# Where the second gate's logits are formed: all 18 row tiles on TensorE, and one table fetch moved behind the writes it reads

## The chip, the cores and the metric

The kernel runs on one core of one Trainium2 chip. The metric is the device time of one execution in microseconds; the time before is the median of three runs. A core has five instruction streams: TensorE (PE, with its weight loads as PEld), VectorE (DVE), ScalarE (ACT), GpSimd (POOL) and SyncE (SP, which issues most DMAs). Each takes its own instructions in the order in which they were issued, and waits at an instruction until what it needs is there.

## The reference, cut to what matters

Three layers follow one another on 2304 rows of 512 values: linear attention, a gated layer of 1536 hidden values, and a mixture of 8 experts of which each row takes one. The change is in the gate of the third layer and in the first expert's rows:

```python
gate = 1.0 / (1.0 + np.exp(-(x @ w_gate)))       # second layer
x = (gate * (x @ w_val)) @ w_out
logits = x @ w_gate                              # third layer: 2304 x 512 by 512 x 8
expert_idx = np.argmax(logits, axis=1)
gate_w = softmax(logits)[np.arange(N), expert_idx]
# rows go to their expert in order, at most `capacity` of them
h = np.maximum(np.einsum('ecd,edf->ecf', disp, w1), 0.0)
y = np.einsum('ecf,efd->ecd', h, w2)
out[i] = gate_w[i] * y[expert_idx[i], pos[i]]
```

## The kernel before, in words

Rows are worked on in six blocks (0 to 5) of 384, each three tiles of 128 rows. Every large product is three matmuls, of a high and a low part of its two operands (`mm3`).

**The loop of the second layer.** A step takes one block and two of the twelve hidden chunks. For each chunk TensorE forms the gate's and the value's sum (`gg` into tile `pg`, `gv` into `pv`), ScalarE the sigmoid (`gs`), VectorE the product with the value (`gm`, L483, tile `sg`), ScalarE and GpSimd its high and low parts (`hh`, L487, and `hl`, L491, tile `h`). Between the two chunks of a step TensorE multiplies the step before's `h` by the output weights (`g2`, tile `po`), and VectorE adds the sums to the rows (L521, tile `acc`) or leaves them open in PSUM for one more step. The last twelve of these steps are called step 0 to 11 here. Block 0 is complete in step 3, block 1 in step 4, block 2 in step 6, block 3 in step 8, block 4 in step 10 and block 5 right behind the loop.

**The gate of the third layer.** A complete block gets its logits, one number for each row and expert. Blocks 0, 1, 2 and two tiles of block 4 get them as sums of products over the row: VectorE sums five of the eight experts itself (`lg_dve`, L557, tiles `jk` and `lg`), GpSimd multiplies the other three (`lg_pool`, L564, tile `jp`) and ScalarE sums them (`lg_sum`, L570). A queue hands these out in steps 3 to 10 (`slot`). Block 3, the last tile of block 4 and block 5, 7 tiles, go to TensorE: `columns` (L780) transposes a row tile in four pieces into `pl`, ScalarE copies it to `w5` (L784), and `logits_mm` (L792, tile `plg`) multiplies by the gate's weights, a few of these matmuls behind each `mm3` of the next chunk (`weave`). Then `route` (L625 to L632) finds each row's expert, `route_b` (L644 to L673) its place in a table with two small matmuls (`pc`) and some twenty small operations of VectorE, and `put` scatters three tiles of entries into the table `tbl` in DRAM (GpSimd, L144). `choose` (L683 to L694) picks the first expert behind block 3, and the first expert's weights (`es`) are fetched from there on.

**Behind the loop** the first expert begins: 192 rows of blocks 0 to 3, gathered in step 10, are multiplied in eight chunks f = 0 to 7, while block 5 is routed (`after0`). Its other 384 rows are gathered at f = 4, and their table rows (`tb`, L160, token and gate weight of each) are used when the results are scaled and scattered at that part's end.

What sets the order of the work around the change is the order in which the code issues it: `at_step(k, j, ...)` puts work at step k, "s" and "t" ahead of the first and the second chunk's matmuls, "m" ahead of `g2`, 0 and 1 behind the first and the second chunk.

Of the kernel before, what the change touches and what calls it, by code (L numbers as in the profile page):

```python
# [8 lines left out]
F32 = mybir.dt.float32  # L9
# [9 lines left out]
P = 128  # L19
# [4 lines left out]
NE = 8  # L24
# [17 lines left out]
# The order in which the work up to the first pair of hidden chunks is issued, each engine's in turn: a step and  # L42
# what it is for (batch, tile or hidden chunk), with a star where VectorE takes it from its usual engine.
# [29 lines left out]
def program(tc, ins, outs):  # L73
    nc = tc.nc
    ctx = ExitStack()
    with ctx:
# [78 lines left out]
        def fetch(st, key, e, r0, k, rest=False):  # L155
            """The table's rows from r0 on: k to a partition, the rest's last half tile in both halves."""
            st[key] = t = tbp.tile([P, k + rest, 4], I32, name=key, tag=key[:2])
            t3 = tbl.rearrange("(e r) w -> e r w", e=NE)
            r1 = r0 + k * P
            nc.sync.dma_start(t[:, :k], t3[bass.ds(e, 1), r0:r1].rearrange("o (p k) w -> (o p) k w", k=k))  # L160
            if rest:
                for h in (0, HALF):
                    rows = t3[bass.ds(e, 1), r1 : r1 + HALF].rearrange("o p w -> (o p) w")
                    nc.sync.dma_start(t[h : h + HALF, k], rows)
# [23 lines left out]
        def part(x, w, sizes, ew, t, ypool, ytag, hook, after):  # L188
            """The rows of one table for one expert. The high and low parts of a tile of half the rows fill the
            array's columns together; the low part's sums then move to the high part's partitions."""  # L190
# [70 lines left out]
        with ExitStack() as s2:  # L261
# [249 lines left out]
            def g2(b, fs, mode):  # L511
                """mode: add (whole sums to SBUF), open and close (a sum over two pairs in PSUM)"""
                order = [(tt, i) for tt in range(TPB) for i in range(2)]
                if b == NBLK - 1 and mode == "close":
                    order = [(tt, 0) for tt in range(TPB)] + [(tt, 1) for tt in range(TPB)]
                for tt, i in order:
                    if i == 0 and mode != "close":
                        otile[b, tt] = pso.tile([P, 512], F32, name=f"po{b}_{fs[0]}_{tt}", tag="o")
                    pair(b, tt, fs[i], i, mode != "close" and i == 0, mode != "open" and i == 1)
                    if i == 1 and mode != "open":  # L520
                        nc.vector.tensor_tensor(row(b, tt), row(b, tt), otile[b, tt], op=ALU.add)  # L521
                if fs[-1] == NFC - 1:
                    finish(b)
# [6 lines left out]
            def open_routing():  # L530
# [3 lines left out]
                wg = p.tile([P, NE, DM], F32, name="wgb", tag="wgb")  # L534
                nc.sync.dma_start(wg, ins["wg"].rearrange("e d -> (e d)").unsqueeze(0).to_broadcast([P, NE * DM]))
                rt["wg"] = wg
# [4 lines left out]
                fill = p.tile([P, NROW // P, 4], I32, name="fill", tag="jp", bufs=2)  # L541
# [12 lines left out]

            def lg_dve(b, tt, e):
                junk = rt["pool"].tile([P, DM], BF16, name=f"jk{b}_{tt}_{e}", tag="junk")
                nc.vector.tensor_tensor_reduce(  # L557
                    junk, row(b, tt), rt["wg"][:, e, :], 1.0, 0.0, op0=ALU.mult, op1=ALU.add,
                    accum_out=rt["lg", b][:, tt, e : e + 1],
                )  # L560

            def lg_pool(b, tt, e):
                prod = rt["pool"].tile([P, DM], F32, name=f"jp{b}_{tt}_{e}", tag="jp", bufs=2)
                nc.gpsimd.tensor_tensor(prod, row(b, tt), rt["wg"][:, e, :], op=ALU.mult)  # L564
                acts.append((b, tt, e, prod))

            def lg_sum(keep):
                while len(acts) > keep:
                    b, tt, e, prod = acts.pop(0)
                    nc.scalar.activation(prod, prod, AF.Copy, accum_out=rt["lg", b][:, tt, e : e + 1])  # L570

            acts, qd, qg, ready = [], [], [], []
            nsum = {0: (5, 5, 5), 1: (5, 5, 5), 2: (5, 5, 5), 4: (5, 5)}

            def logits(b):
                """Queues the logits of block b: DVE sums nsum[b] products of a row, Pool and ScalarE the others."""
                lg_tile(b)
                for tt, n in enumerate(nsum[b]):
                    qd.extend((b, tt, e) for e in range(n))
                    qg.extend((b, tt, e) for e in range(n, NE))  # L580

            def slot(room, spare):
                """Fills the time that DVE (room, in products) and Pool (spare) have until the next pair's turn."""
                lg_sum(0)
                put = None
                busy = {x[0] for x in qd + qg}
                for b in [b for b in range(3) if ("lg", b) in rt and b not in busy]:
                    route(b)
                    ready.append(b)
                    room -= 2  # L590
                    break
                else:
                    if room > 4 and ready:
                        put = route_b(ready.pop(0))
                        room, spare = room - 5, spare - 3
                while room > 0 and qd:
                    lg_dve(*qd.pop(0))
                    room -= 1
                while spare > 0 and qg:
                    lg_sum(1)  # L600
                    lg_pool(*qg.pop(0))
                    spare -= 1
                if put is not None:
                    put()
# [171 lines left out]

            def columns(b, tt):
                pt = ps(f"pl{b}_{tt}")
                for c in range(NC):
                    nc.tensor.transpose(pt[:, c * P : (c + 1) * P], row(b, tt)[:, c * P : (c + 1) * P], ident)  # L780
                if tt == 1 and b == NBLK - 1:
                    nc.vector.tensor_copy(w5[:, 0, tt], pt)
                else:
                    nc.scalar.copy(w5[:, 0, tt], pt)  # L784

            def logits_mm(b, tts, then=None):
                if tts[0] == 0:
                    lg_tile(b)
                pl = ps(f"plg{b}")

                def one(tt, c):
                    nc.tensor.matmul(  # L792
                        pl[:, tt * NE : (tt + 1) * NE],
                        w5[:, 0, tt, c * P : (c + 1) * P],
# [5 lines left out]
                def end():  # L800
                    s = slice(tts[0] * NE, TPB * NE)
                    nc.vector.tensor_copy(rt["lg", b].rearrange("p t e -> p (t e)")[:, s], pl[:, s])
                    if then is not None:
                        then()

                n = 2 if b == 3 else 3
                pairs = [(tt, c) for tt in tts for c in range(NC)]
# [25 lines left out]
            for b, k in ((0, 3), (1, 4), (2, 6), (4, 10)):  # L833
                at_step(k, 0, lambda b=b: logits(b))
            for k in range(3, 9):
                at_step(k, 0, lambda k=k: slot(9 if k > 3 and k % 2 else 7, 5))
                at_step(k, 1, lambda: slot(4, 2))
            at_step(8, 1, lambda: [columns(3, tt) for tt in range(TPB)])
# [3 lines left out]
            at_step(9, "s", lambda: logits_mm(3, range(TPB), lambda: route(3)))  # L842
            at_step(9, "m", lambda: late("put2", lambda: route_b(ready.pop(0))))
            at_step(9, 0, lambda: rt["put2"](), choose, dma(0), dma(1), lambda: late("put3", lambda: route_b(3)))
            at_step(9, 1, lambda: rt["put3"]())
            at_step(10, 0, first_table, split(0), dma(2), lambda: slot(6, 5))
            at_step(10, "t", lambda: weave.extend([lambda: None] * 4 + [lambda: columns(4, 2)]))
            at_step(10, 1, lambda: slot(4, 1), split(1), dma(3), first_rows)
            at_step(11, "s", lambda: logits_mm(4, [2]))
            at_step(11, 0, lambda: lg_sum(0), lambda: route(4), split(2), dma(4))  # L850
# [3 lines left out]
            for i, (b, fs, mode) in enumerate(steps):  # L854
# [28 lines left out]
                if i == n4 + 7:  # L883
                    w5 = unit([P, 2, TPB, DM], F32, "w5")
# [17 lines left out]
            def last_rows():  # L902
# [12 lines left out]
                def end():  # L915
# [3 lines left out]
                    rt["put"]()  # L919

                weave.extend([lambda: None] + [lambda k=k: one(k) for k in range(3)] + [end])

            def after0(f):
                if f == 0:
# [4 lines left out]
                    logits_mm(b5, range(TPB), lambda: route(b5))  # L929
# [6 lines left out]
                if f == 3:  # L936
                    last_rows()
                    ew_split(ew0, 7, both)
                    fetch(st0, "tb", rt["e0"], R0, 3)
# [119 lines left out]
def layout(inputs):  # L1059
# [14 lines left out]
    wg = np.ascontiguousarray(inputs["moe2_w_gate"].T)  # L1074
    wgt = np.ascontiguousarray(inputs["moe2_w_gate"].reshape(NC, P, NE).transpose(1, 0, 2))
    cap = np.asarray(inputs["moe2_capacity"]).astype(np.int64).reshape(1)
    return {"q": q, "v": v, "kT": kT, "w": w, "w1": w1, "w2": w2, "wg": wg, "wgt": wgt, "cap": cap}
# [20 lines left out]
```

## Time and profile before

| | us |
|---|---|
| median of three runs | 813.92 |
| lowest and highest | 813.45, 814.21 |
| span of the profiled execution, first to last instruction | 815.9 |
| TensorE busy in that span | 757.5 (93%) |
| VectorE, GpSimd, ScalarE busy | 474.4 (58%), 321.0 (39%), 293.0 (36%) |

The profile is of one execution, and its time is given by the span alone; that is 2.0 us above the median. TensorE is busy nearly throughout, so the places to read are those in which it isn't, and what it waits for there.

### The profile page before, as it was taken

The numbers are of one execution on the slowest core, as the hardware profiler recorded it, in microseconds if no ns is written. First come the engines' busy times: TensorE is split into PE (matmuls) and PEld (weight loads), VectorE is DVE, ScalarE is ACT, GpSimd is POOL, SyncE is SP. The second block draws the span as 40 slices with busy tenths as digits, with TensorE's granted clock in tenths as the row PEclk, the third lists the DMA queues.
The fourth block names the chain that finished last, engine by engine and source line by source line (L and its number), as shares of the span: only waits on it lengthen the run. The fifth ranks groups of instructions, "written<-read, shape, count | busy, mean of one in ns | idle before, by whom it ended". The sixth has DMA issues, their size and how long they took to land. (4 is left out here: it accounts for less than half of the span.)

```text
span 815.9 us, 11856 instructions
## 1 busy us (share of the span) xinstructions
PE 757.5 (93%) x4268; PEld 689.0 (84%) x4268; DVE 474.4 (58%) x933; ACT 293.0 (36%) x592; POOL 321.0 (39%) x309
## 2 busy tenths in 40 slices
PE   6989999999999999999997898989999999999980
PEld 5988998999999999999886787978798888888870
DVE  7999956344545445546889895587624422533330
ACT  6766733222222222222333332233235433523330
POOL 5472703222323223223466763462435423425220
PEclk9999999999999999999999898999999999999995
DMA  9951023101101011011211011124245523415311
GB/s 308 365 174 58 27 78 130 57 26 52 50 29 52 28 50 52 27 53 51 79 39 40 1 39 40 53 91 144 66 146 189 177 78 125 155 53 176 129 46 30
DMA packets 34942, 72.62 MB, mean 89 GB/s; under 512 B 6544, under 2 KB 8720, under 8 KB 34736
## 3 DMA queue, kind: packets, MB, share of 16 engines
q1 hardware_dynamic: 31152, 61.50, 22.7%
q0 software_dynamic: 3712, 10.13, 3.8%
q8 instruction: 42, 0.69, 0.4%
q14 instruction: 36, 0.29, 0.1%
HBM read 61.55 MB, written 9.55 MB: 87 GB/s over the span
## 5 line engine op out<-in xcount | busy, mean ns | idle before, releaser
L491 POOL TENSOR_TENSOR h<-sg,h 128x384 fp32r<-128x384 f32 x70 | 77.7, 1111 | 200.8 <-ACT h L487 194.6
L483 DVE TENSOR_TENSOR sg<-sg,pv 128x384 f32<-128x384 f32 x72 | 39.6, 551 | 103.2 <-PE pv L117 78.5
L115 PE MATMUL po<-w,h 128*128 128x512 f32 x216 | 88.4, 409 | 10.9 <-ACT h L487 10.9
L117 PE MATMUL pv<-xT,w 128*128 128x384 f32 x288 | 97.1, 337 | 1.5 <-POOL w L451 1.5
L115 PE MATMUL pg<-xT,w 128*128 128x384 f32 x288 | 98.0, 340 | 0.0
L115 PE MATMUL pv<-xT,w 128*128 128x384 f32 x288 | 97.7, 339 | 0.1
L116 PE MATMUL pv<-xT,w 128*128 128x384 f32 x288 | 96.8, 336 | 0.0
L116 PE MATMUL pg<-xT,w 128*128 128x384 f32 x288 | 96.7, 336 | 0.0
L117 PE MATMUL pg<-xT,w 128*128 128x384 f32 x288 | 96.4, 335 | 0.0
L117 PE MATMUL po<-w,h 128*128 128x512 f32 x216 | 89.4, 414 | 4.5 <-POOL h L491 4.4
L116 PE MATMUL po<-w,h 128*128 128x512 f32 x216 | 87.6, 406 | 0.0
L238 DVE SCALAR_TENSOR_TENSOR h<-ph,h 128x64 fp32r<-128x64 f32 (+2 forms) x96 | 31.3, 353 | 94.6 <-ACT h L235 87.5
L451 POOL TENSOR_TENSOR w<-cv,w 128x512 fp32r<-128x512 f32 x34 | 45.0, 1324 | 98.7 <-ACT w L447 97.7
L487 ACT CAST h<-sg 128x384 fp32r<-128x384 f32 x68 | 34.9, 514 | 132.9 <-DVE sg L483 125.0
L135 POOL TENSOR_TENSOR eu<-es,eu 128x512 fp32r<-128x512 f32 x34 | 44.4, 1310 | 87.1 <-ACT eu L134 80.9
L521 DVE TENSOR_TENSOR acc<-acc,po 128x512 f32<-128x512 f32 x78 | 52.8, 686 | 34.7 <-PE po L117 32.7
L479 ACT ACTIVATE sg<-pg 128x384 f32<-128x384 f32 x72 | 35.0, 486 | 102.8 <-PE pg L117 102.8
L235 ACT ACTIVATE h<-ph 128x256 fp32r<-128x256 f32 (+3 forms) x64 | 26.3, 411 | 109.0 <-PE ph L117 54.4
L135 DVE TENSOR_TENSOR eu<-es,eu 128x512 fp32r<-128x512 f32 x46 | 48.3, 1061 | 26.3 <-ACT eu L134 26.0
L115 PEld LDWEIGHTS po<-w,h 128*128 128x128 f32 x216 | 42.0, 194 | 21.3 <-ACT h L487 13.5
L557 DVE CUSTOM_DVE_ANT_0 jk<-acc,wgb 128x512 bf16<-128x512 f32 x55 | 58.8, 1069 | 1.5
L117 PEld LDWEIGHTS po<-w,h 128*128 128x128 f32 x216 | 42.3, 196 | 17.3 <-POOL h L491 7.4
(206 smaller groups left out, 1804.1 us busy)
## 6 DMA issues: line engine op xcount, KB each, us to landing
es<-in_w SPq DMA_DIRECT2D x80, 256.0 KB
s<-in_w SPq DMA_DIRECT2D x30, 512.0 KB
q<-in_q SPq DMA_DIRECT2D x18, 256.0 KB
x2d<-acc SPq DMA_DIRECT2D x6, 768.0 KB
kt<-in_kT SPq DMA_DIRECT2D x3, 1152.0 KB
vt<-in_v SPq DMA_DIRECT2D x3, 1024.0 KB
raw<-in_w SPq DMA_DIRECT2D x6, 512.0 KB
wgb<-in_wg SPq DMA_DIRECT2D x1, 2048.0 KB
```

The lines of the kernel that those rows point to most:

```text
L115: nc.tensor.matmul(out, l_hi, r_hi, start=start, stop=False)
L116: nc.tensor.matmul(out, l_hi, r_lo, start=False, stop=False)
L117: nc.tensor.matmul(out, l_lo, r_hi, start=False, stop=stop)
L135: engines[(i + f) % 2].tensor_tensor(u[:, 1], s[:, i], u[:, 0].bitcast(F32), op=ALU.subtract)
L238: nc.vector.scalar_tensor_tensor(dst, ph[:, cols], 0.0, h[:, 0, cols].bitcast(F32), op0=ALU.max, op1=ALU.subtract)
L451: two[eng].tensor_tensor(w[:, i, 1, :], ld.pop(("c", f, i))[0], w[:, i, 0, :].bitcast(F32), op=ALU.subtract)
L479: nc.scalar.activation(pr, gt.pop(("g", b, f)), AF.Sigmoid)
L483: nc.vector.tensor_tensor(pr, pr, gt.pop(("v", b, f)), op=ALU.mult)
L487: alt[eng](h[:, 0], gt["r", b, f])
L491: two[eng].tensor_tensor(h[:, 1], gt.pop(("r", b, f)), h[:, 0].bitcast(F32), op=ALU.subtract)
L521: nc.vector.tensor_tensor(row(b, tt), row(b, tt), otile[b, tt], op=ALU.add)
L557: nc.vector.tensor_tensor_reduce(junk, row(b, tt), rt["wg"][:, e, :], 1.0, 0.0, op0=ALU.mult, op1=ALU.add, accum_out=rt["lg", b][:, tt, e ...
```

## The change

All 18 row tiles now take the way of the 7: `columns` puts the transposes of a complete block behind step 3, 4, 6, 8 and 10, and the logits' matmuls of the block are woven into the next step's first chunk, with `route` behind them, `route_b` behind that step's `g2` and `put` behind its second chunk. `lg_dve`, `lg_pool`, `lg_sum`, `slot` and the copy of the gate's weights on all partitions (`wgb`, 2 MB, fetched at the loop's start) are gone. `w5` is taken six steps earlier, and block 4 uses its second half. `choose` now stands behind block 3's `route_b`. The fetch of `tb` moves from f = 3 to behind the last `put`.

```diff
-            for b, k in ((0, 3), (1, 4), (2, 6), (4, 10)):
-                at_step(k, 0, lambda b=b: logits(b))
-            for k in range(3, 9):
-                at_step(k, 0, lambda k=k: slot(9 if k > 3 and k % 2 else 7, 5))
-                at_step(k, 1, lambda: slot(4, 2))
-            at_step(8, 1, lambda: [columns(3, tt) for tt in range(TPB)])
...
-            at_step(9, "s", lambda: logits_mm(3, range(TPB), lambda: route(3)))
-            at_step(9, "m", lambda: late("put2", lambda: route_b(ready.pop(0))))
-            at_step(9, 0, lambda: rt["put2"](), choose, dma(0), dma(1), lambda: late("put3", lambda: route_b(3)))
-            at_step(9, 1, lambda: rt["put3"]())
-            at_step(10, 0, first_table, split(0), dma(2), lambda: slot(6, 5))
-            at_step(10, "t", lambda: weave.extend([lambda: None] * 4 + [lambda: columns(4, 2)]))
-            at_step(10, 1, lambda: slot(4, 1), split(1), dma(3), first_rows)
-            at_step(11, "s", lambda: logits_mm(4, [2]))
-            at_step(11, 0, lambda: lg_sum(0), lambda: route(4), split(2), dma(4))
+            for b in range(5):
+                k = (4, 5, 7, 9, 11)[b]
+                at_step(k - 1, 1, lambda b=b: [columns(b, tt) for tt in range(TPB)])
+                at_step(k, "s", lambda b=b: logits_mm(b, lambda: route(b)))
+                if b < 4:
+                    at_step(k, 0, lambda b=b: late("put", lambda: route_b(b)))
+                    at_step(k, 1, lambda: rt["put"]())
+            at_step(9, 0, choose, dma(0), dma(1))
+            at_step(10, 0, first_table, split(0), dma(2))
+            at_step(10, 1, split(1), dma(3), first_rows)
+            at_step(11, 0, split(2), dma(4))
             at_step(11, "t", lambda: weave.extend([lambda: None] * 2 + [lambda: late("put4", lambda: route_b(4))]))
...
-                if i == n4 + 7:
                     w5 = unit([P, 2, TPB, DM], F32, "w5")
...
                     for i in range(3):
                         gather(st0, 2 + i, gidx[:, i : i + 1], w5[:, 0, i], P)
                     rt["put"]()
+                    fetch(st0, "tb", rt["e0"], R0, 3)
...
                 if f == 3:
                     last_rows()
                     ew_split(ew0, 7, both)
-                    fetch(st0, "tb", rt["e0"], R0, 3)
```

VectorE before, from step 3's second chunk (`sg_11`) to step 4's first (`sg_8`); `jk` are products for the logits of block 0:

```order
L483 TENSOR_TENSOR sg_11_3727<-sg_11_3727,pv_11_3714 128x384
L557 ISA jk_1_2_3735,lg_3673<-acc_1036,wgb 128x512
L557 ISA lg_3673 128x1
L557 ISA jk_1_3_3737,lg_3673<-acc_1036,wgb 128x512
L557 ISA lg_3673 128x1
L557 ISA jk_1_4_3739,lg_3673<-acc_1036,wgb 128x512
L557 ISA lg_3673 128x1
L557 ISA jk_2_0_3741,lg_3673<-acc_1036,wgb 128x512
L557 ISA lg_3673 128x1
L483 TENSOR_TENSOR sg_8_3773<-sg_8_3773,pv_8_3760 128x384
```

VectorE with the change, at the same place:

```order
L483 TENSOR_TENSOR sg_11_3698<-sg_11_3698,pv_11_3685 128x384
L749 COPY lg_3722<-plg_3723 128x24
L571 TENSOR_REDUCE s_3762<-lg_3722 128x3
L572 TENSOR_TENSOR wk_3760<-lg_3722,s_3762 128x24
L573 TENSOR_TENSOR wk_3760<-wk_3760,iotm 128x24
L574 TENSOR_REDUCE s_3762<-wk_3760 128x3
L575 TENSOR_TENSOR oh_3761<-iotm,s_3762 128x24
L578 TENSOR_TENSOR run<-run,oh_3761 128x8 x3
L483 TENSOR_TENSOR sg_8_3779<-sg_8_3779,pv_8_3745 128x384
```

Four products over 512 columns stood ahead of `sg_8`; now the copy of the logits and the eight operations of `route` over at most 24 columns stand there.

TensorE with the change, where step 3 ends and step 4 begins; before, the first `pg_8` followed the last `pv_11` at once:

```order
L116 MATMUL pv_11_3685<-xT_335,w_3503 128x384
L117 MATMUL pv_11_3685<-xT_335,w_3503 128x384
L729 MATMUL pl_0_3704<-ident,acc_1036 128x128 x4
L729 MATMUL pl_1_3710<-ident,acc_1036 128x128 x4
L729 MATMUL pl_2_3716<-ident,acc_1036 128x128 x4
L115 MATMUL pg_8_3724<-xT_770,w_2796 128x384
L116 MATMUL pg_8_3724<-xT_770,w_2796 128x384
L117 MATMUL pg_8_3724<-xT_770,w_2796 128x384
L740 MATMUL plg_3723<-wgt,w_3526 128x8 x2
L115 MATMUL pg_8_3724<-xT_770,w_2796 128x384
```

Twelve transposes stand between the two chunks, and the logits' matmuls, two behind each `mm3`, follow.

SP before, in the first expert's part; `tb` is the fetch that the change moves, `z` a copy of results that VectorE adds:

```order
L124 DMA es_5096<-in_w 128x512
L160 ISA
L160 DMA tb<-tbl 128x12
L217 DMA z_5349<-y_5347 64x512 [waits Activation_49]
L973 TENSOR_LOAD plan [waits DVE_49]
```

SP with the change, at the same place:

```order
L124 DMA es_5001<-in_w 128x512
L160 ISA
L160 DMA tb<-tbl 128x12 [waits DMASW6_49]
L217 DMA z_5254<-y_5252 64x512 [waits Activation_49]
L914 TENSOR_LOAD plan [waits DVE_49]
```

The fetch keeps its place in SP's queue and gains a wait, for the landing of the last scatter that GpSimd issued into the table; the copy of `z` stands behind it.

## Rows read from the trace of the kernel before

**Rows 1.** Page, busy tenths of TensorE in 40 equal slices of the span

```profile
PE   6989999999999999999997898989999999999980
```

**Rows 2.** Steps 3, 7, 9, 10, 11 and their stretch, windows; columns in the first row

```profile
core 0: us, PE busy (x) PEld busy (x) DVE busy (x) ACT busy (x) POOL busy (x), PEclk, DMA share, GB/s
406.93:419.48 12.55, 12.55 (x67) 11.73 (x67) 8.69 (x12) 5.34 (x14) 10.27 (x9) 1.00 0.17 63
...
471.71:486.78 15.07, 13.24 (x69) 11.54 (x69) 14.48 (x33) 4.28 (x13) 8.77 (x11) 1.00 0.00 0
...
505.76:522.82 17.06, 17.06 (x108) 15.67 (x107) 9.01 (x50) 3.80 (x9) 4.38 (x8) 1.00 0.03 6
522.82:535.83 13.01, 13.01 (x71) 12.16 (x71) 7.48 (x10) 5.60 (x13) 11.24 (x11) 1.00 0.42 135
535.83:555.66 19.83, 15.67 (x78) 13.78 (x78) 17.43 (x51) 5.93 (x15) 7.06 (x9) 0.93 0.32 102
406.93:555.66 148.73, 130.89 (x655) 116.09 (x655) 119.86 (x287) 45.61 (x121) 83.89 (x82) 0.93 0.14 48
```

**Rows 3.** Lines of TensorE, 406.93 to 555.66: busy, mean ns, idle before, releasers

```profile
L117 PE MATMUL po<-w,h 128*128 128x512 f32 x54 | 25.0, 463 | 4.5 <-POOL h L491 4.4
L115 PE MATMUL po<-w,h 128*128 128x512 f32 x54 | 24.4, 453 | 10.9 <-ACT h L487 10.9
...
L644 PE MATMUL pc<-oh,tri 128*128 128x24 bf16 x5 | 0.9, 182 | 2.2 <-DVE oh L629 2.2
```

**Rows 4.** Lines of VectorE and GpSimd, same stretch: the logits' products

```profile
L557 DVE CUSTOM_DVE_ANT_0 jk<-acc,wgb 128x512 bf16<-128x512 f32 x55 | 58.8, 1069 | 1.5
...
L564 POOL TENSOR_TENSOR jp<-acc,wgb 128x512 f32<-128x512 f32 x33 | 47.0, 1452 | 0.0
```

**Rows 5.** Timeline of VectorE in step 5: start us, us, line, tiles

```profile
439.34 1.63 DVE L557 CUSTOM_DVE_ANT_0 jk<-acc,wgb 128x512 bf16<-128x512 f32 x1
...
441.01 0.69 DVE L557 CUSTOM_DVE_ANT_0 jk<-acc,wgb 128x512 bf16<-128x512 f32 x1
...
442.36 0.55 DVE L483 TENSOR_TENSOR sg<-sg,pv 128x384 f32<-128x384 f32 x1
```

**Rows 6.** Timeline of TensorE in step 5, its wait in brackets

```profile
443.51 0.61 PE L115 MATMUL po<-w,h 128*128 128x512 f32 x1 [4.78 <-ACT h L487]
```

**Rows 7.** Window of TensorE behind that wait: us, busy, granted clock

```profile
443.51:447.26 3.75, 3.70 (x9) 0.54 0.00 0
```

**Rows 8.** Tile plg: what its instructions waited for, us and times

```profile
  ACT w L784: 0.2, 1
```

**Rows 9.** Timeline of VectorE in step 9

```profile
513.15 0.18 DVE L802 COPY lg<-plg 128x24 f32<-128x24 f32 x1 [6.57 <-PE plg L792]
...
514.92 0.55 DVE L483 TENSOR_TENSOR sg<-sg,pv 128x384 f32<-128x384 f32 x1
...
520.16 0.16 DVE L653 TENSOR_TENSOR wk<-pc,oh 128x24 f32<-128x24 f32 x1
...
523.48 0.54 DVE L483 TENSOR_TENSOR sg<-sg,pv 128x384 f32<-128x384 f32 x1
```

**Rows 10.** Timelines of SP and ScalarE: the first expert's first weights

```profile
521.35 0.29 SPq L123 DMA_DIRECT2D es<-in_w  x1
...
528.26 1.14 ACT L134 CAST eu<-es 128x512 fp32r<-128x512 f32 x2
```

**Rows 11.** Timelines of GpSimd, SP and VectorE: scatters, table fetches, z

```profile
561.79 0.97 POOL L144 DMA_INDIRECT tbl<-ent,si  x1 [0.30 <-issue]
...
565.12 0.33 SPq L160 DMA_DIRECT2D tb<-tbl  x1
...
587.67 0.98 POOL L144 DMA_INDIRECT tbl<-ent,si  x1 [0.30 <-issue]
...
592.12 0.51 SPq L217 DMA_DIRECT2D z<-y  x1
...
595.19 0.68 DVE L219 TENSOR_TENSOR y<-y,z 64x512 f32<-64x512 f32 x1 [2.13 <-DMA z<-y]
```

More of the change, by code (lines that the diff above doesn't have):

```diff
@@ L533, in open_routing @@
                 rt["pool"] = p
-                wg = p.tile([P, NE, DM], F32, name="wgb", tag="wgb")
-                nc.sync.dma_start(wg, ins["wg"].rearrange("e d -> (e d)").unsqueeze(0).to_broadcast([P, NE * DM]))
-                rt["wg"] = wg
                 rt["wgt"] = wgt = p.tile([P, NC, NE], F32, name="wgt", tag="wgt")
@@ L540, in open_routing @@
                 rt["rel"] = p.tile([P, TPB], F32, name="rel", tag="rel")
-                fill = p.tile([P, NROW // P, 4], I32, name="fill", tag="jp", bufs=2)
+                fill = p.tile([P, NROW // P, 4], I32, name="fill", tag="fill")
                 nc.gpsimd.memset(fill, 0)
@@ L553, in lg_tile @@
                 rt["lg", b] = rt["pool"].tile([P, TPB, NE], F32, name=f"lg{b}", tag="lg", bufs=2)
[L555 to L604, printed above, removed]
             def route(b):
@@ L775, in program, with side @@
             w5 = None
+            def side(b):
+                return int(b == 4)
             def columns(b, tt):
@@ L781, in columns, with logits_mm @@
                 if tt == 1 and b == NBLK - 1:
-                    nc.vector.tensor_copy(w5[:, 0, tt], pt)
+                    nc.vector.tensor_copy(w5[:, side(b), tt], pt)
                 else:
[L784 to L788, printed above, removed]
+                    nc.scalar.copy(w5[:, side(b), tt], pt)
+            def logits_mm(b, then):
+                rt["lg", b] = rt["pool"].tile([P, TPB, NE], F32, name=f"lg{b}", tag="lg", bufs=2)
                 pl = ps(f"plg{b}")
@@ L793, in one @@
                         pl[:, tt * NE : (tt + 1) * NE],
-                        w5[:, 0, tt, c * P : (c + 1) * P],
+                        w5[:, side(b), tt, c * P : (c + 1) * P],
                         rt["wgt"][:, c, :],
@@ L800, in end @@
                 def end():
[L801 to L807, printed above, removed]
+                    nc.vector.tensor_copy(rt["lg", b].rearrange("p t e -> p (t e)"), pl[:, : TPB * NE])
+                    then()
+                n = 3 if b > 3 else 2
+                pairs = [(tt, c) for tt in range(TPB) for c in range(NC)]
                 for i in range(0, len(pairs), n):
@@ L928, in after0 @@
                     dma(6)()
-                    logits_mm(b5, range(TPB), lambda: route(b5))
+                    logits_mm(b5, lambda: route(b5))
                 if f == 1:
@@ L1073, in layout @@
     w2 = np.ascontiguousarray(inputs["moe2_w2"]).reshape(NE, 8, P, DM)
-    wg = np.ascontiguousarray(inputs["moe2_w_gate"].T)
     wgt = np.ascontiguousarray(inputs["moe2_w_gate"].reshape(NC, P, NE).transpose(1, 0, 2))
     cap = np.asarray(inputs["moe2_capacity"]).astype(np.int64).reshape(1)
-    return {"q": q, "v": v, "kT": kT, "w": w, "w1": w1, "w2": w2, "wg": wg, "wgt": wgt, "cap": cap}
+    return {"q": q, "v": v, "kT": kT, "w": w, "w1": w1, "w2": w2, "wgt": wgt, "cap": cap}
 def kernel(**inputs):
```

## The prediction

> **What bounds the kernel now.** I read the page's slices first: TensorE is full in nearly all of them, but a little past the middle, in some six slices, sevens and eights stand between the nines [rows 1]. Windows cut at the steps give the size of it. Step 3 takes 12.55 us, with TensorE busy in all of them at full clock; steps 3 to 11 together take 148.73 instead of 9 x 12.55 = 112.95 us [rows 2]. That is 35.8 us more. Part of it is work: the stretch from the transposes of block 3 through step 9 takes 17.06 us without any idle time, 4.51 more than a plain step, and that is the price of one block's logits, routing and choice of the first expert on TensorE [rows 2]. With a third of it for the one tile of block 4, 6.0 us are work. The other 29.8 are lost: 148.73 - 130.89 = 17.8 idle [rows 2], and 148.73 - 17.8 - 112.95 - 6.0 = 12.0 in which TensorE works at its lower clock.
>
> The lines tell what it waits for: the two parts of `h`, 10.9 us for ScalarE's and 4.5 for GpSimd's, and 2.2 us for VectorE's `oh` ahead of the small matmuls `pc` [rows 3]. ScalarE and GpSimd are not late by themselves. Both follow VectorE's product `sg`, and ahead of that in VectorE's queue stand the sums for the logits: 55 of them, 58.8 us in this stretch, beside 33 products on GpSimd, 47.0 us [rows 4]. One sum takes 0.69 us, and 1.63 while GpSimd multiplies too; in step 5 a row of them ends with `sg` at 442.36 [rows 5], and TensorE, which had waited 4.78 us, goes on at 443.51 [rows 6]. The next 3.75 us run at a granted clock of 0.54, the lower of the two levels, 1.2 and 2.4 GHz [rows 7]; against full clock that loses (1 - 0.54) x 3.75 = 1.7 us. A wait of this length is paid again in part.
>
> **The change part by part.** *Removed:* the 55 sums and 33 products of [rows 4], with ScalarE's 33 sums and the broadcast copy of the gate's weights. Nothing of these is on TensorE; their removal is worth what TensorE waits because of them. I take all 29.8 us as theirs, since the one step of this stretch that has logits and two routings but no such sum, step 9, has no idle time, and step 10 behind it, where a late `h` of step 9 would show, has none either [rows 2].
>
> *Added on TensorE:* blocks 0, 1, 2 and 4 now cost what block 3 costs, 4.51 us for three tiles. That is 5 x 4.51 = 22.6 us where 6.0 were. It is on the path in full, since nothing else fills TensorE less for it. Four of the five have one pair of `pc` matmuls fewer than step 9 and no choice; that makes 22.6 an upper end, and I leave it there.
>
> *Moved on VectorE.* In a step with logits the copy and `route` now stand ahead of the first chunk's `sg`, and `route_b` ahead of the second's. In step 9 the first pair lasted from 513.15 to 514.92, 1.8 us, and `route_b` from 520.16 to 523.48, 3.3 us [rows 9]. A step is 66 matmuls, and each of its thirds (first chunk, `g2`, second chunk) has 9216 columns, so a third is 12.55 / 3 = 4.18 us. `route_b` begins when `g2` ends and has 4.18 us until the second chunk's `sg` can begin at all: it fits with 0.9 to spare. In step 4 alone the last of three additions stands in front too; it then fits by about 0.2, and as the transposes of block 1 follow that `sg` through ScalarE, half a microsecond may be lost there. The handover itself, `sg`, `h`, three copies, first logits' matmul, has little slack: in step 9 TensorE's weight load waited 0.2 us for ScalarE's copy [rows 8]. From that row I take nothing beyond the 4.51, which holds it; at the other end stands step 7, where a late `h` cost 15.07 - 12.55 = 2.5 us without loss of clock [rows 2]. So the five handovers cost 0 to 12.6 us more.
>
> *Choice of the first expert.* It now follows block 3's `route_b`, 3.3 us later. Its first weights were asked for at 521.35 and cast at 528.26, 6.9 us later [rows 10]. Asked for 3.3 later they are cast by 531.6, and VectorE's two subtractions after it (a sum of the same size takes 0.69 [rows 5]) end ahead of step 10's second `sg`, due at 522.82 + 12.55 = 535.4 on the same clock. Cost nothing, with over 1 us of cover; behind that it would be one for one.
>
> *Step 11.* `route` of block 4 moves from behind `g2` into the first chunk, so `oh` is there a third of a step before `pc` wants it; the 2.2 us of [rows 3] go, and they are in the 29.8. Next late is the second `sg`, with `route_b` of block 4 in front, as before.
>
> *The moved fetch of `tb`.* It waits for the third scatter of block 5, which GpSimd ended at 587.67 + 0.98 = 588.65 [rows 11]. How long it takes such a scatter to land is shown by the fetch of the earlier table, which started at 565.12, 2.4 us after the scatter in front of it ended at 561.79 + 0.97 = 562.76 [rows 11]. So SP goes on at about 591.0. What is queued behind it is the copy of `z`, issued at 592.12 [rows 11]: 1.1 us of cover. If that were gone, VectorE, which already waits 2.13 us for `z` with the next `h` behind it [rows 11], would wait longer, one for one; I bound that by another 2.1. The rows of `tb` themselves are used only at the end of the part that begins there, after eight chunks. I take nothing.
>
> **The sum.** 148.73 - 112.95 - 22.6 = 13.2 us gained. In the profiled execution 815.9 becomes 802.7. The median of the runs lies 2.0 us under that span, and I carry the difference over: 813.92 - 13.2 = 800.7 us, 1.6% faster.
>
> **A rule against it.** TensorE ran the transposes of block 3 and all of step 9 at a granted clock of 1.00 [rows 2]. The Trainium skill, "TensorE: Matmul & The Clock Gate", section "Part 4: PE-mode transpose", says that the higher clock does not engage for transposes. By that rule the time would come out as in the second rival; the row does not bear it out.
>
> **The rivals.**
> *Handover late (0.13).* Five times in this stretch TensorE reaches the logits' matmuls before ScalarE has copied. For it speaks the slack of 0.2 us [rows 8], against it that step 9 shows no more than that with two routings in it. Between 0.2 and 2.5 us each, say 1.3, makes 6.5: 807.2 us.
> *Clock lost at transposes (0.03).* If twelve transposes in a row left the matmuls behind them at the lower level, as a wait does, that would be five times 1.7 us [rows 7], 8.6 in all: 809.3 us. Against it stands the 1.00 of [rows 2].
> *The waits were not the sums' (0.05).* The place is VectorE's queue ahead of `sg`: if some twenty short operations of `route` and `route_b`, each waiting for the one before, hold up `h` as the sums did, the 29.8 us stay and TensorE has 16.6 us more to do: 813.92 + 16.6 = 830.5 us, slower. It decides from the point where more than 13.2 of the 29.8 stay. For it: sums and routing stood in the same steps, so the waits alone do not tell them apart. Against it: step 9 [rows 2], and that GpSimd has little left to do beside VectorE.
> That the products go from VectorE and GpSimd is in the order itself, so no rival is made of it.
>
> **How the numbers follow.** My forecast has 0.79; its own range is 797.5 to 803 (a block for a tenth less than 4.51 gives 2.3 us, a little more comes if the start of the first expert meets a free VectorE; step 4's half microsecond and the two of `tb` lie on the other side). To hold 8 in 10 I go up to the middle of the late handover: 797.5 to 807.2. Some 0.2% (1.6 us) is about what a measurement of this kernel can tell from no change. Faster by more: the forecast, the clock, and the handover but for its uppermost end, 0.93. Within: that end, where the handovers take 12 us, 0.02. Slower: the third rival, 0.05.
>
> **What would show it.** In the changed kernel's trace steps 3 to 11 take about 135.5 us, the waits of `po` for `h` are under 2 us in all, and the granted clock of that stretch is at least 0.98. VectorE is busy for under half of it (119.86 - 58.8 = 61 us by [rows 2, 4]). Steps 4, 5, 7, 9 and 11 last some 4.5 us more than the others, with their transposes. From the first expert's start to the end the trace lasts as long as before, 815.9 - 555.66 = 260.2 us, within 1 us, and `z` is issued as soon as ScalarE has written `y`. I am wrong if `po` still waits for `h` in the steps with routing, if weight loads of `plg` wait for ScalarE by more than 1 us each, if the clock falls behind the transposes, or if the gain of the stretch is given back behind it.

## The result, and the profile after

The changed kernel took 800.26 us (median of 4 runs, 798.98 to 800.67) against 813.84 (4 runs, 813.45 to 814.21): a ratio of 0.9835, with a 95% interval of 0.9823 to 0.9847. The profiled execution took 800.0 us with a span of 798.2. In a few executions, of the kernel before too, the mean granted clock was 0.75 or lower and the time over 100 us longer; all times and ratios here leave these out.

The sevens and eights of [rows 1] are gone from the page's slices of TensorE:

```profile
PE   6989999999999999999999999999999999999980
```

Steps 3, 4, 7, 9, 10, 11 and the whole stretch, as windows with the columns of [rows 2]:

```profile
406.75:419.30 12.55, 12.55 (x67) 11.71 (x67) 5.43 (x9) 3.31 (x8) 4.33 (x4) 1.00 0.17 63
419.30:436.17 16.87, 16.87 (x106) 15.59 (x104) 7.33 (x32) 3.58 (x8) 2.23 (x5) 1.00 0.13 48
465.66:482.52 16.86, 16.86 (x105) 15.62 (x104) 5.37 (x29) 3.69 (x8) 2.23 (x5) 1.00 0.00 1
495.07:512.05 16.98, 16.98 (x107) 15.74 (x105) 6.11 (x35) 3.69 (x8) 2.22 (x5) 1.00 0.00 1
512.05:524.60 12.55, 12.55 (x68) 11.70 (x68) 4.44 (x9) 3.06 (x6) 5.04 (x5) 1.00 0.46 148
524.60:541.52 16.92, 16.92 (x105) 15.69 (x104) 7.86 (x30) 5.66 (x12) 4.34 (x7) 1.00 0.40 126
406.75:541.52 134.77, 134.77 (x786) 125.14 (x786) 48.24 (x181) 30.72 (x66) 35.91 (x49) 1.00 0.16 54
```

The stretch of 148.73 us lasts 134.77; TensorE is busy in all of it, at a granted clock of 1.00 where it was 0.93. A step with logits costs 4.3 to 4.4 us more than a plain one. The lines of `po`, which had waited 15.3 us for `h` [rows 3], have no wait left. What is left is a short wait of the weight loads of `plg` for ScalarE's copies, 0.2 us in each of the five steps:

```profile
L117 PE MATMUL po<-w,h 128*128 128x512 f32 x54 | 21.5, 398 | 0.0
...
L115 PE MATMUL po<-w,h 128*128 128x512 f32 x54 | 21.2, 393 | 0.0
...
L740 PEld LDWEIGHTS plg<-wgt,w 128*128 128x128 f32 x120 | 17.0, 190 | 1.1 <-ACT w L733 1.1
```

Behind the loop the trace shows something that was not forecast. Timelines of GpSimd, SP, ScalarE, VectorE and TensorE at the end of the first expert's first part, in order of time (the answers to [rows 11]):

```profile
573.17 0.98 POOL L144 DMA_INDIRECT tbl<-ent,si  x1 [0.30 <-issue]
...
575.29 1.29 ACT L214 ACTIVATE y<-yo,ta 128x512 f32<-128x512 f32 x2
...
577.92 0.33 SPq L160 DMA_DIRECT2D tb<-tbl  x1
578.63 0.51 SPq L217 DMA_DIRECT2D z<-y  x1
...
581.00 0.68 DVE L219 TENSOR_TENSOR y<-y,z 64x512 f32<-64x512 f32 x1 [4.65 <-DMA z<-y]
...
582.21 0.50 PE L117 MATMUL yo<-eu,h 128*128 128x512 f32 x1 [1.70 <-DVE h L238]
```

The third scatter ends at 574.15; the moved fetch goes out 3.8 us later, not 2.4. It goes out when the scatter has landed, 4.7 us after that was issued (the last number, us from issue to landing):

```profile
tbl<-ent,si POOLq DMA_INDIRECT x1, 4.7
```

ScalarE's first `y` is written at about 576.0, and its copy `z`, queued behind the fetch, leaves 2.6 us after that. VectorE waits for `z`, the next `h` stands behind its addition, and TensorE waits 1.70 us for that `h`.

### The profile page after: what moved, and what is told of

It is laid out like the page before. It is cut to its first block, busy times and chain, and to the rows that moved or that the text cites. A ratio compares the mean times of both kernels' runs of the same rounds, so it can differ in the third digit from the quotient of the medians.

```text
span 798.2 us, 11945 instructions
## 1 busy us (share of the span) xinstructions
PE 759.5 (95%) x4400; PEld 698.0 (87%) x4400; DVE 402.2 (50%) x826; ACT 278.8 (35%) x537; POOL 273.2 (34%) x276
## 5 line engine op out<-in xcount | busy, mean ns | idle before, releaser
L117 PE MATMUL po<-w,h 128*128 128x512 f32 x216 | 86.0, 398 | 0.0
L115 PE MATMUL po<-w,h 128*128 128x512 f32 x216 | 85.2, 394 | 0.0
L116 PE MATMUL po<-w,h 128*128 128x512 f32 x216 | 85.1, 394 | 0.0
L135 DVE TENSOR_TENSOR eu<-es,eu 128x512 fp32r<-128x512 f32 x46 | 43.1, 948 | 32.7 <-ACT eu L134 32.3
L117 PEld LDWEIGHTS pv<-xT,w 128*128 128x128 f32 x288 | 54.1, 188 | 2.2 <-POOL w L451 2.2
L116 PEld LDWEIGHTS pg<-xT,w 128*128 128x128 f32 x288 | 54.2, 188 | 1.3
L115 PEld LDWEIGHTS pg<-xT,w 128*128 128x128 f32 x288 | 54.1, 188 | 1.4
```

The costliest lines, as they stand in the source:

```text
L115: nc.tensor.matmul(out, l_hi, r_hi, start=start, stop=False)
L116: nc.tensor.matmul(out, l_hi, r_lo, start=False, stop=False)
L117: nc.tensor.matmul(out, l_lo, r_hi, start=False, stop=stop)
L135: engines[(i + f) % 2].tensor_tensor(u[:, 1], s[:, i], u[:, 0].bitcast(F32), op=ALU.subtract)
```

## The experiments

The numbers are those of the runs; there is no run 9. A ratio is that of the mean times, the profiled execution left out, to the kernel before executed beside it, with its 95% interval.

**1 and 2. The moved fetch.** The first puts it back to f = 3; the second leaves it behind the scatters, but takes it out of `z`'s way, to the start of the first expert's second part (`part` then asks for the tile when it first scales results).

```diff
# 1
-                    fetch(st0, "tb", rt["e0"], R0, 3)      # behind put
+                    fetch(st0, "tb", rt["e0"], R0, 3)      # at f == 3
# 2
-                    fetch(st0, "tb", rt["e0"], R0, 3)
...
         def extra0(f):
+            if f == 0:
+                fetch(st0, "tb", rt["e0"], R0, 3)
```

> The changed kernel with one part undone: the fetch of tb is issued at f = 3 again, so it does not wait for block 5's three scatters (block 5's rows of the first expert are then not among the table rows that it brings, and those results are left out). As the prediction has it, the moved fetch costs nothing: 800.3 us as the changed kernel, within 0.5. By the trace of the changed kernel the fetch held SyncE until 577.92, 3.8 us after the third scatter, z left 2.6 us after y was written, and po's successor yo waited 1.70 us: then the time falls by 1.7 to 2.0 us, to some 798.4, and z is issued within 0.3 us of y's end.

> The changed kernel with the fetch of tb still behind the scatters, but issued in SyncE's queue behind the copy z, at the start of the first expert's second part. If what costs is that z stands behind a waiting fetch, the time is that of the kernel with the early fetch, some 798.4 us, with all results formed. If the cost came from the scatters and the fetch taking DMA time from z, it stays near 800.3. As the prediction has it (no cost): 800.3.

Measured: 799.33 (6 runs, 797.91 to 803.78; 0.9837 of before, 0.9806 to 0.9868) and 800.41 (5 runs, 797.30 to 801.10; 0.9837, 0.9808 to 0.9866). By the times neither can be told from the changed kernel's 0.9835, so the 1.7 to 2.0 us that I expected are not shown by them. In the traces the wait of 1.70 us is gone in both; in experiment 3, which leaves the fetch where the change put it, it is there again with 1.43 us. SP and VectorE of the second:

```profile
576.46 0.51 SPq L220 DMA_DIRECT2D z<-y  x1
...
578.81 0.68 DVE L222 TENSOR_TENSOR y<-y,z 64x512 f32<-64x512 f32 x1 [2.03 <-DMA z<-y]
```

`z` leaves as soon as `y` is written, and VectorE waits 2.03 us, not 4.65. So what made the wait was the place in SP's queue. One reason why the times need not show it stands a little earlier, at f = 4, where TensorE waits 0.50 us for an `h` in both kernels. First the changed kernel, TensorE's wait in the timeline and a window behind it, then the same two of experiment 1 (in a window the granted clock is the third number from the end):

```profile
564.53 0.50 PE L117 MATMUL yo<-eu,h 128*128 128x512 f32 x1 [0.50 <-DVE h L238]
```

```profile
564.53:567.50 2.97, 2.97 (x19) 2.49 (x20) 2.63 (x10) 0.33 (x1) 1.75 (x2) 1.00 0.00 0
```

```profile
564.59 0.80 PE L117 MATMUL yo<-eu,h 128*128 128x512 f32 x1 [0.50 <-DVE h L238]
```

```profile
564.59:567.93 3.34, 3.34 (x12) 2.63 (x13) 2.63 (x10) 0.00 (x0) 1.84 (x2) 0.51 0.00 0
```

The same wait was followed by the lower clock in one execution and not in the other, which is (1 - 0.51) x 3.34 = 1.6 us. That is as much as the fetch costs, and it comes and goes. A step of 1.7 us here is read from a trace, not from such times. (That the clock made up the difference in the executions without a profile is not shown.)

**3. The handover.** Logits' matmuls of blocks 0 to 4 begin one `mm3` later.

```diff
                 pairs = [(tt, c) for tt in range(TPB) for c in range(NC)]
+                if b < 5:
+                    weave.append(lambda: None)
```

> The changed kernel with the logits' matmuls of blocks 0 to 4 begun one mm3 later, so that ScalarE's three copies of the transposes have some 0.5 us more. In the changed kernel the weight loads of plg waited 1.1 us for them in all, some 0.2 in each of five steps. If TensorE loses that, the time falls by up to 1.1 us to some 799.2, and those waits go; if the loads' waits are covered by matmuls still running, or route then comes late, it stays at 800.3 or rises.

Measured: 799.05 us (0.9824, 0.9799 to 0.9850), which the times alone can't tell from the changed kernel. Step 4's first chunk and `g2`, and the whole stretch; then the former of the changed kernel:

```profile
421.07:432.27 11.20, 11.20 (x72) 10.20 (x69) 3.33 (x12) 2.60 (x6) 2.24 (x5) 1.00 0.01 1
407.29:541.10 133.81, 133.81 (x787) 125.33 (x787) 48.11 (x181) 30.73 (x66) 35.97 (x49) 1.00 0.16 54
```

```profile
420.53:431.91 11.38, 11.38 (x71) 10.14 (x70) 3.42 (x12) 2.61 (x6) 2.23 (x5) 1.00 0.01 1
```

The stretch is 134.77 - 133.81 = 0.96 us shorter, of the 1.1 that the loads waited, and that wait is gone from the trace. So in the changed kernel the handover was late, by 0.2 us a block.

**4. Twice the transposes.**

```diff
-                for c in range(NC):
+                for c in list(range(NC)) * (2 if b < 5 else 1):
                     nc.tensor.transpose(...)
```

> The changed kernel with the transposes of blocks 0 to 4 done twice each, 24 in a row instead of 12; nothing else differs. If a transpose costs TensorE only its own time (12 took some 1.2 us) and keeps the higher clock, the time rises by 5 x 1.2 = 6 us to some 806.3 and the granted clock of the steps stays at 1.00. If a row of transposes lets the clock fall (the prediction's second rival, 1.7 us a place), it rises by up to 14.5 to some 815 and the windows behind them show a lower granted clock.

Measured: 804.11 us (0.9884, 0.9858 to 0.9910). The second chunk of step 3 with the transposes behind it, in this kernel and in the changed one:

```profile
414.91:421.63 6.72, 6.72 (x49) 6.69 (x48) 1.24 (x2) 2.08 (x4) 1.09 (x3) 1.00 0.31 117
```

```profile
415.11:420.53 5.42, 5.42 (x37) 5.38 (x36) 1.24 (x2) 0.86 (x2) 0.00 (x0) 1.00 0.39 145
```

Twelve transposes cost 1.30 us and the clock stays at 1.00. The stretch is 140.37 us, 5.6 more: 5 x 1.30 less the handover's wait, which goes here too. The time rose by less, 3.9 us. With that agrees that in this profile the third scatter landed sooner, the fetch went out 1.1 us behind the scatter's end, and nothing waited for `z`:

```profile
tbl<-ent,si POOLq DMA_INDIRECT x1, 2.1
```

**5, 10 and 11. The kernel before with its sums cut short.** In experiment 5 on both engines, in 10 on VectorE alone, in 11 on GpSimd and ScalarE alone.

```diff
-                    junk, row(b, tt), rt["wg"][:, e, :], 1.0, 0.0, ...
+                    junk[:, :64], row(b, tt)[:, :64], rt["wg"][:, e, :64], 1.0, 0.0, ...   # 5, 10
-                nc.gpsimd.tensor_tensor(prod, row(b, tt), rt["wg"][:, e, :], op=ALU.mult)
+                nc.gpsimd.tensor_tensor(prod[:, :64], row(b, tt)[:, :64], rt["wg"][:, e, :64], op=ALU.mult)   # 5, 11
...
-                    nc.scalar.activation(prod, prod, AF.Copy, ...)
+                    nc.scalar.activation(prod[:, :64], prod[:, :64], AF.Copy, ...)   # 5, 11
```

> The kernel before with every sum on VectorE and every product on GpSimd over 64 of the 512 columns, in the same places of the queues. The logits of blocks 0, 1, 2 and of two tiles of block 4 so leave out seven eighths of each row, the routing differs, and what comes behind the loop is not comparable; what counts is steps 3 to 11, 148.73 us before. If the waits are the sums', they go: 112.95 + 6.0 = about 119 us, with full clock. If they are the routing's (the third rival), which stays as it was with the same number of operations, the stretch stays near 148.

> The kernel before with VectorE's 55 sums over 64 of the 512 columns, GpSimd's products whole. The logits leave out seven eighths of the rows for five experts, so only steps 3 to 11 count: 148.73 us before, 119.3 with both engines' work short. If the waits are VectorE's queue alone, 119 to 123 us. If GpSimd's products, which stand ahead of its part of h, and ScalarE's sums behind them hold up h by themselves, over 126.

> The counterpart: the kernel before with GpSimd's 33 products and ScalarE's sums over 64 of 512 columns, VectorE's 55 sums whole. Only steps 3 to 11 count. If what makes VectorE late is that GpSimd slows its sums (0.69 us alone, 1.63 beside a product), they now fit between the products sg: 119 to 124 us. If 55 sums at 0.75 us are too many by themselves, over 130.

Steps 3 to 11 of the three, in this order:

```profile
407.01:526.30 119.29, 119.29 (x655) 110.69 (x655) 63.26 (x287) 34.37 (x121) 45.68 (x82) 1.00 0.18 61
```

```profile
407.00:533.75 126.75, 122.18 (x654) 111.64 (x654) 87.23 (x283) 45.27 (x119) 77.17 (x82) 0.99 0.16 53
```

```profile
407.07:526.83 119.76, 119.55 (x654) 110.58 (x654) 89.19 (x284) 33.30 (x121) 49.44 (x82) 1.00 0.17 57
```

Without the sums the stretch takes 119.29 us, with all of the routing in its place; 118.95 was worked out. The waits were the sums'. VectorE's whole sums alone bring 0.5 us of the loss back, GpSimd's whole products alone 7.5, and both together 29.4 (27.0 by the second profile of the kernel before, experiment 13). So the larger part, 21.4 us (19.0 by that profile), comes of the two at once. Each of the three is one execution. The lines of VectorE's whole sums in 11, and of GpSimd's whole products in 10, beside the 1069 and 1452 ns of [rows 4]:

```profile
L557 DVE CUSTOM_DVE_ANT_0 jk<-acc,wgb 128x512 bf16<-128x512 f32 x55 | 41.8, 760 | 1.5
```

```profile
L564 POOL TENSOR_TENSOR jp<-acc,wgb 128x512 f32<-128x512 f32 x33 | 41.7, 1293 | 0.0
```

What remains with GpSimd's products alone are waits for its own part of `h`, which stands behind them (engine and line, what it waited for, us, times, longest):

```profile
PE po L117 <- POOL h L491: 3.9, 3, 2.0
```

The rows show how the two hold each other up. A sum takes 0.69 us with GpSimd idle and 1.63 beside a product [rows 5]. Five products in a row took 8.06 us beside the sums of step 5 in the kernel before, and 6.30 in experiment 10, whose sums are short:

```profile
432.36 8.06 POOL L564 TENSOR_TENSOR jp<-acc,wgb 128x512 f32<-128x512 f32 x5
```

```profile
426.57 6.30 POOL L564 TENSOR_TENSOR jp<-acc,wgb 128x512 f32<-128x512 f32 x5
```

The Trainium skill, "SBUF — State Buffer", section "SBUF: two separate sides", says that VectorE and GpSimd have a pair of ports in common, and that a VectorE instruction with two inputs in SBUF, as the sums are, and a GpSimd instruction that reads SBUF can't have it at once: one holds it for its whole instruction while the other stands still. The rows agree in part: a product beside the sums took 8.06 / 5 = 1.61 us, more than the 1.26 of experiment 10, but less than the 1.26 + 0.69 = 1.95 that one behind the other would take.

**6 to 8. The sums put back into the changed kernel.** At the places of the queues where they had stood, with what they form used by nothing, and with the copy of the weights that they read (`wgb`): in 6 all, in 7 VectorE's, in 8 GpSimd's and ScalarE's.

```diff
+            for b, k in ((0, 3), (1, 4), (2, 6), (4, 10)):
+                at_step(k, 0, lambda b=b: sums_of(b))
...
+            for k in range(3, 12):
+                for j in range(2):
+                    at_step(k, j, lambda k=k, j=j: sums(plan_v.get((k, j), 0), plan_g.get((k, j), 0)))
```

> The changed kernel with the 55 sums of VectorE, the 33 products of GpSimd and ScalarE's 33 sums put back at the places of the queues where they stood before; what they form is used by nothing, so the routing is the same. If the waits were the sums', they come back beside TensorE's own logits: up to 29.8 us more, somewhat less since five steps are 4.3 us longer, so 818 to 830 us, slower than the kernel before. If the sums alone delay nothing and before it was sums and routing in one slot, below 808.

> As the one with the sums put back, but with VectorE's 55 alone, without GpSimd's products and ScalarE's sums. If a sum takes 0.69 us whenever GpSimd doesn't multiply, seven take 4.8 us of the 8.4 between two products sg and four take 2.8 of 4.2: all fits, and the time stays at 800 to 803. If 55 sums are too many even by themselves, the most part of the waits is here: over 812.

> As the one with the sums put back, but with GpSimd's 33 products and ScalarE's 33 sums alone. If the waits come only of the two engines slowing one another, this costs no more than 3 us (800 to 803): five products stand ahead of GpSimd's part of h. If GpSimd is late by itself, since its part of h stands behind five products of 1.4 us, 805 to 815, with waits of po for GpSimd's h.

Measured: 857.34 us (1.0536, 1.0517 to 1.0555), 824.46 (820.88 to 826.33; 1.0137, 1.0111 to 1.0163) and 819.66 (3 runs, 815.41 to 824.59; 1.0101, 1.0059 to 1.0142). 6 and 8 lie above every range that I had named. 7 lies in the range that I had given for sums that are too many even by themselves, which experiment 11 speaks against. Their stretches, of which those of 7 and 8 are from the shortest execution of each:

```profile
406.65:598.67 192.02, 161.87 (x786) 149.44 (x786) 115.17 (x290) 51.72 (x132) 81.39 (x82) 0.80 0.12 38
```

```profile
406.81:561.06 154.25, 145.74 (x786) 135.65 (x786) 87.87 (x290) 30.50 (x66) 37.62 (x49) 0.92 0.14 47
```

```profile
407.32:558.49 151.17, 144.73 (x786) 134.14 (x786) 55.14 (x181) 51.73 (x132) 77.15 (x82) 0.93 0.14 48
```

The same work costs 57.3 us where it cost 27 to 29, VectorE's part alone 19.5 where it cost 0.5, and GpSimd's 16.4 where it cost 7.5. One difference is what waits: no longer `po`, but for the most part the logits' matmuls, which need ScalarE's copies `w`. First the wait of TensorE in experiment 7's stretch (us, times, longest), then TensorE at the start of step 4, then VectorE, ScalarE and TensorE up to the start of step 5, in order of time:

```profile
PE plg L743 <- ACT w L736: 8.5, 4, 4.2
```

```profile
422.63 0.61 PE L743 MATMUL plg<-wgt,w 128*128 128x8 f32 x4 [1.27 <-ACT w L736]
...
434.07 0.18 DVE L602 TENSOR_TENSOR wk<-pc,oh 128x24 f32<-128x24 f32 x1
...
437.09 0.18 DVE L622 RECIPROCAL ent<-s 128x3 f32<-128x3 f32 x1
...
441.56 0.69 DVE L817 CUSTOM_DVE_ANT_0 jk<-acc,wgb 128x512 bf16<-128x512 f32 x1
...
442.18 0.55 DVE L483 TENSOR_TENSOR sg<-sg,pv 128x384 f32<-128x384 f32 x1
...
442.76 0.51 ACT L487 CAST h<-sg 128x384 fp32r<-128x384 f32 x1 [6.50 <-DVE sg L483]
443.18 1.55 ACT L736 COPY w<-pl 128x512 f32<-128x512 f32 x3
...
443.81 1.02 PE L743 MATMUL plg<-wgt,w 128*128 128x8 f32 x4 [4.22 <-ACT w L736]
```

Sums ahead of `sg` make it late; ScalarE's `hh` waits for `sg`, and behind it stand the copies of the transposes, which TensorE needs in the chunk that follows at once. In the kernel before, `sg` of a second chunk was wanted only by the next step's `g2`, a third of a step later. The handover has made VectorE's queue a part of TensorE's path. A second difference is in VectorE's queue itself: the change routes a block one step earlier, so in step 4 `route_b` (434.07 to 437.27) now stands ahead of the same seven sums, which it didn't before. TensorE waits 4.22 us behind both, and 1.27 us at the start of step 4, where sums stand without routing. So part of the 19.5 us is of sums and routing in one slot, and how much each of the two differences makes is not shown. In experiments 8 and 6 TensorE also waits, for 3.1 and 6.6 us, for ScalarE's sigmoid `sg`, ahead of which ScalarE's sums stand.

**12. Three edits together.** Experiments 2 and 3, and the weights' subtraction that stands ahead of `h` at f = 4 moved to GpSimd.

```diff
-                    ew_split(ew0, 6, both)
+                    ew_split(ew0, 6, (nc.gpsimd, nc.gpsimd))
```

> The changed kernel with three edits: the fetch of tb behind z, the logits' matmuls one mm3 later, and both subtractions of the first expert's seventh weight pair on GpSimd, which idles there, so that VectorE's h at f = 4 is not behind one. By the traces: 1.7 us for the wait of yo at the second part's start, 1.0 for the five handovers, 0.5 for the wait at f = 4, and with it a fall of the clock that takes 1.5 us in some executions: 3 to 4 us less than the changed kernel, 796 to 797.5. If such waits are only moved on to the next late thing, 799 or more.

Measured: 796.62 us (5 runs, 796.55 to 797.11), 0.9802 of before (0.9789 to 0.9816); the interval lies below that of the changed kernel. The waits at f = 4 and at the second part's start are gone, and its stretch and what lies behind it are 133.81 and 254.38 us. It beats both kernels.

**13. The kernel before, once more.** Nothing is edited.

> The kernel before once more, with a profile, nothing edited. In its first profile the part behind the loop lasted 260.3 us, in that of the changed kernel 256.7. If that difference is one execution's, the stretch of steps 3 to 11 is again 148.7 within 0.5 and the part behind it 254 to 258.5 us, as in the other profiles of the changed kernel's family; if the change shortened it, it is again 259.5 to 261.

Measured: 812.78 us (1.0009, 0.9995 to 1.0024), with a profile of a span of 809.4, the shortest of its ten executions. Its stretch and its part behind the loop, and then the latter of the changed kernel:

```profile
406.41:552.67 146.26, 130.09 (x655) 115.42 (x655) 119.12 (x284) 45.00 (x119) 83.86 (x82) 0.93 0.14 46
552.67:809.40 256.73, 233.19 (x1380) 205.94 (x1378) 99.07 (x232) 93.17 (x186) 93.86 (x85) 0.96 0.37 118
```

```profile
541.52:798.20 256.68, 231.56 (x1380) 204.76 (x1378) 98.28 (x227) 92.11 (x184) 93.53 (x85) 0.96 0.37 116
```

The 260.3 us of the first profile were one execution's: the same code took 256.7 here. The stretch, too, moves by 2.5 us from one execution to the next, which I had not expected.

The two executions also tell what the cover of the moved fetch was made of. Behind TensorE's wait of 0.51 us at f = 4 the clock stayed at 1.00 in the first, and ScalarE's last `h` of the part was late:

```profile
579.02:582.50 3.48, 3.48 (x21) 2.88 (x22) 3.14 (x13) 0.33 (x1) 1.95 (x3) 1.00 0.00 0
```

```profile
589.72 0.33 ACT L235 ACTIVATE h<-ph 128x192 fp32r<-128x192 f32 x1 [5.17 <-PE tg L181]
```

In the second the clock fell there, and `z` left 3.4 us after the third scatter ended, as it had left 3.5 us after it in the first:

```profile
576.75:580.20 3.45, 3.45 (x13) 2.73 (x14) 2.65 (x10) 0.00 (x0) 1.92 (x3) 0.51 0.00 0
```

```profile
585.40 0.98 POOL L144 DMA_INDIRECT tbl<-ent,si  x1 [0.31 <-issue]
...
589.79 0.51 SPq L217 DMA_DIRECT2D z<-y  x1
```

Where neither happened, in the changed kernel and in experiment 2, `y` was written some 1.9 us after it; in experiment 1, where the clock fell as well, 3.4 us.

## Why the prediction was right, point by point

- *The waits are the sums'.* Shown: with short sums the stretch falls to 119.29 us where the reckoning was 118.95, with clock and idle time both back (experiment 5). The third rival, that the routing holds up `h`, is out by this. What I had told of VectorE's queue alone was half of it: the loss is mostly of the two engines together (10, 11). The 12.0 us put down to the lower clock were a remainder; by the granted clock of [rows 2] some (1 - 0.93) x 130.89 = 9.2 us of them are shown.
- *Five blocks at 4.51 us.* 134.77 - 112.95 = 21.8 us, 4.4 a block, against 22.6; I had named 4.51 an upper end. Of it 1.3 are the transposes (4) and 0.2 the handover's wait (3); the rest, the logits' and the routing's matmuls, no run parts further.
- *The handover.* As read from [rows 8], which shows a wait of 0.2 us and no slack: 0.2 us five times, and no more, so the first rival's 1.3 us did not come. That nothing covers it is shown by 6 to 8, where it turns lateness of VectorE and ScalarE into TensorE's at once.
- *Clock at the transposes.* Stays at 1.00, with twelve in a row and with 24 (4). The second rival is out.
- *VectorE, choice, step 11.* VectorE is busy for 48.2 us of the stretch; I forecast 61. The 58.8 us of sums go and 4.4 of reading their totals, which I had not counted, and other operations take less time now: the weights' subtractions `eu` 4.3 us instead of 8.4, the additions `run` 2.4 instead of 6.6. Step 10 takes 12.55 us without a wait, so the later choice costs nothing, and in step 11 nothing waits.
- *The moved fetch of `tb`, taken at nothing: wrong.* The step that failed is the cover of 1.1 us, with 2.4 us to land. The fetch left 3.8 us after the scatter, and `y` was written 1.9 us after it, where [rows 11] had `z` issued 3.5 us after. The size of both terms was off. The landing is not of one length: the same scatter took 4.7 us from its issue in the changed kernel, and 2.1 in experiments 1 and 4 and in the second execution of the kernel before. And the 3.5 us held some 1.6 us of lateness, behind ScalarE's last `h` of that part, which the changed kernel's execution didn't have. A second execution of the kernel before would not have warned: there `z` leaves 3.4 us after the scatter's end too, for another reason (13). TensorE lost 1.70 us, within the 2.1 that I had bounded (1, 2). What made `h` late in the first execution is open.
- *Behind the loop 260.2 us within 1.* Wrong, since that length was one execution's (13).
- *The sum.* The stretch gained 14.0 us against the first profile of before and 11.5 against the second, where 13.2 were forecast; the medians differ by 13.6. Against the 800.7 forecast, 800.26 came out; the fetch's 1.7 and the blocks' 0.8 are of opposite sign, and both are of the size by which executions differ. So that it came within 0.4 us is in part luck. In addition, a time is 1.8 us longer than its span (800.0 and 798.2, 811.16 and 809.4), so the execution profiled first took some 817.7 us, by estimate, 3.8 above the median and not 2.0; its stretch of 148.73 us is the longer of the two measured.

## What to carry to other kernels

Price a queue's work by what it takes while the other engine works too: two engines that cost little alone can be late together, and the bounding engine may do the work itself for less than it lost by waiting. Before a wait is put into a DMA queue, look at what stands behind it, and ask what the cover is made of: lateness and a lower clock can be gone in the next execution, even where two traces show them. Work woven straight into the bounding engine's next step makes the queues that feed it critical; here beginning it one slot later brought 1.0 us.

## What was not expected of the hardware

- The same wait of TensorE, 0.50 us, was followed by 3.34 us at a granted clock of 0.51 in one execution and by 1.00 in another (experiment 1 and the changed kernel; in experiment 2 it didn't fall either). Two executions of the kernel before differ in the same way: behind a wait of 0.51 us the clock was 1.00 in the first and 0.51 for 3.45 us in the second, which is 1.7 us.
- A fetch that waits for three indirect scatters left 3.8 us after the last of them ended on GpSimd in the changed kernel and 1.1 us after it in experiment 4. The last scatter had taken 4.7 and 2.1 us from its issue to land. Why its landing differs so is open.
- VectorE's sums and GpSimd's products slow one another, though not alike: a sum from 0.76 us to 1.07 in the mean, a product from 1.29 to 1.45. Side by side they still take less than one behind the other would (1.61 us for a product, against 1.95).
